# Local attention in groups of 32 queries: 64x32 and 128x32 TensorE tiles in place of 64x128 and 128x64

## The chip, the cores and the metric

One core of a Trainium2 chip runs the whole program. The metric is the device time of one execution in microseconds (us); the times shown are medians of several runs, and one further execution was profiled.

## What is computed

A block of attention feeds two feed-forward layers, all in fp32. Of 544 tokens in each of 4 batches, 32 are global and see every key, and 512 are local and see the 32 global keys and the local keys within 32 positions. There are 8 heads of 64.

```python
window, scale = 32, 1.0 / np.sqrt(D)                  # B, H, Sl, Sg, D = 4, 8, 512, 32, 64
sm = lambda s: e / (e.sum(-1) + 1e-9)                 # with e = exp(s - max(s))
out_g = sm(scale * q_g @ k_all.T) @ v_all             # k_all, v_all: global, then local
s_ll = where(abs(i - j) <= window, scale * q_l @ k_l.T, -1e9)
out_l = sm(concat(scale * q_l @ k_g.T, s_ll)) @ concat(v_g, v_l)
x = concat(out_g, out_l) as [2176 tokens, 512]
h = maximum(x @ w1_in, 0); x = (h * h) @ w1_out       # 512 -> 2048 -> 512
h = maximum(x @ w2_in, 0); out = (h * h) @ w2_out
```

## The kernel before

**Two stages.** First comes attention, with the first of the feed-forward work let in between; from about 168 us on there is feed-forward work alone. A feed-forward product is made of three fp32r matmuls, high by high, high by low and low by high parts (`three`, lines 580 to 583), of 384 or 512 moving columns each; the weights and activations are split into such parts by ScalarE (high) and VectorE (low).

**Local attention** is done by `pair(j)`, 32 times: two heads (e = 0, 1) of 256 queries, as two tiles (t = 0, 1) of 128 queries with 224 keys each (96 local ones, the 32 global ones, 96 local ones). For each pair the steps are these. (1) Three loads, issued by SyncE: keys `rk`, queries `rq` and values `vt` (two buffers). (2) `scores`: 4 matmuls of 64 rows by 128 columns with 224 moving keys, the two heads on the two halves of the rows, into banks S0 and S1. (3) On VectorE a custom operation adds the mask, scales, and takes the minimum (line 339), in 4 pieces; on ScalarE the exponential with the sum read out of the accumulator (line 344), in 4 pieces. (4) `tiny` turns the sums into reciprocals, and 4 passes over 224 columns multiply the weights by them (`copy("nm", ...)`, five of six on VectorE). (5) `trans`: 8 transposes on TensorE, of 128x128 and 96x96; ScalarE evicts them in 4 copies into `pt`. (6) `pv`: 8 matmuls of 64 columns with the weights moving (128 or 96 queries), the sum over keys in two parts (128 and 96 of them), into bank O0. It comes out transposed, as the feed-forward layer wants it. (7) `split_out` splits it into `xh` (ScalarE) and `xl` (VectorE).

An fp32 matmul of the code leaves two records in the trace, a transpose one.

**Global attention** is done by `glob(bb)`, four times: `scores` twice (line 425: 8 matmuls of 64x32, 272 moving keys), 11 transposes, and `pv` (line 475: 40 matmuls of 128x32 and 32x32, 64 values moving). Its keys and values are 2.5 MB of loads (`kg`, `y`).

**What sets the order.** All operations are first handed to `Plan`, which simulates them with booked costs and priorities (`add(engine, cost, priority, ...)`) and writes each engine's instructions in the order found. So costs, the `CFG` numbers and the buffer counts set the order, and each engine then runs its list strictly. SyncE issues the loads in list order too: one that waits for its buffer holds up those behind it.

**PSUM** has 8 banks: h0, h1, S0, S1, Y0, PT0, PT1 (transposes) and O0 (products with values).

**Weights** come as 8-byte numbers: `weight` loads 512 KB into one raw buffer and rebuilds fp32 on VectorE in 4 passes and one of AND (line 507) or, 5 times in 8, of Abs on ScalarE. **Activation** of hidden units (`activate`, line 590) of staged sums is relu, square and square again on ScalarE, or for one in six (`gs`) one VectorE pass and one ScalarE copy.

Of the kernel before, what the change touches and what calls it, by code (L numbers as in the profile page):

```python
# [17 lines left out]
S = SG + SL  # L18
# [6 lines left out]
NEAR = 96  # L25
# [10 lines left out]
CFG = {'warm': 27,  # L36
 'sg': 'A',
 'tl': 'DDDDD',
 'EARLY': 8,
 'nm': 'DDDADD',  # L40
 'ev': 'A',
 'yc': 'AAA',
 'wl': 'D',
 'gl': 'D',
 'xh': 'AA',
 'glob': [5.9, 15.73, 25.15, 42.23],
 'w0': 26.27364175797601,
 'w1': 9.640861192642154,
 'moe': [65.961, 79.468, 82.888, -1123.016, 96.609],
 'step': [0.0012, 0.0036, 0.0016, 0.0125, 0.102],  # L50
 'NK': 3,
 'NQ': 5,
 'wa': 'DAAAADDA',
 'lid': -5.887,
 'lmk': -15.028,
 'lead': 15.411,
 'NM': 1,
 'NS': 5,
 'NPT': 3,
 'NV': 2,  # L60
 'NR': 7,
 'NWR': 1,
 'NWT': 4,
# [3 lines left out]
 'PT': ['PT0', 'PT1'],  # L67
 'O': ['O0'],
 'tp': [215.87, 786.002, 884.208, 247.503],
 'order': ['A0B', 'BA0', 'AB0', 'A0B', 'AB0', '0BA', 'B0A', 'A0B', 'A0B', 'A0B', 'BA0', 'A0B', 'BA0', 'BA0'],  # L70
 'NSLOT': 9,
 'NGS': 2,
 'gf': 'A',
 'gs': 'AAAADA',
# [110 lines left out]

def switch(a, b):

    if a in "SVWX":
        return 0.0 if a == b else 0.095 if b in "SVWX" else 0.205 if b in "MG" else 0.145
    return 0.092 if b in "SVWX" else 0.012 if a != b else 0.0  # L190
# [10 lines left out]
def pe_r(n, m=128):  # L201
    return max(n + 32, 2 * m + 6) / 2400
# [3 lines left out]
def kernel(ctx: ExitStack, tc: tile.TileContext, kl, ql, vl, gk, gv, win, wout, msk, idn, out):  # L206
# [87 lines left out]
    cnt = {"S": 0, "PT": 0, "g": 0, "h": 0, "Y": 0, "r": 0, "x": 0}  # L294
# [10 lines left out]
    def pair(j, prio):  # L305
        u, h2 = divmod(j, H // 2)
        kb, qb, vb = j % NK, j % NQ, j % NV
# [7 lines left out]
        K, Q = ("rk", kb), ("rq", qb)  # L315
# [3 lines left out]
        load(prio - lead + 0.5, vt[vb], vl[j], 262144, A, (("v", vb),))  # L319
# [10 lines left out]
        add("PE", 0.77, P(), scores, A + (K, Q), tuple(sk), mode="S")  # L330
        pbs = []
        ok = CFG["O"][j % len(CFG["O"])]
        mb = j % NM
        for e in range(2):
            sb, s = (2 * j + e) % NS, sk[e]
            for t in range(2):
                qt = (u % 2) * 2 + t
                mi = 0 if qt == 0 else (2 if qt == 3 else 1)
                add("DVE", 0.32, P(), lambda t=t, mi=mi, sb=sb, s=s: nc.vector.tensor_tensor_reduce(  # L339
                    out=st[sb][:, t, :], in0=bank[s][:, t * WIN:(t + 1) * WIN], in1=masks[:, mi, :],  # L340
                    op0=ALU.add, op1=ALU.min, scale=-0.125, scalar=3.0e38, accum_out=mn[sb][:, t:t + 1]),
                    A + (s, "masks"), (("s", sb, t), ("mn", sb, t)))
            for t in range(2):
# [459 lines left out]
    for j in range(NI // 2):  # L803
        pair(j, 2 * j)
        for g, at in enumerate(GPOS):
            if at // 2 == j:
                glob(g, at + 0.5)
# [139 lines left out]
```

## Time and profile before

| | us |
|---|---|
| median of 3 runs (854.95 to 856.67) | 855.0 |
| the profiled execution | 854.51 |
| its span | 852.7 |
| TensorE busy | 842.1 (99%) |
| VectorE busy | 668.6 (78%) |
| ScalarE busy | 520.8 (61%) |
| load and store queues | 22.8% of 16 engines |

Busy time of TensorE is the union of records whose ends overlap the next one's start, so work is better read from start to start of neighbouring records. Rows of the timeline merge equal instructions that follow each other: "x16" is 16 records, and the second number is from the first start to the last end. The window view gives the busy time of each engine in a stretch, the granted TensorE clock (1.00 is 2.4 GHz), the mean busy share of the 16 DMA engines, and GB/s. The releaser named in brackets is what ended an idle time.

### The profile page before, as it was taken

What the parts mean: (1) busy time and instruction counts of PE and PEld (TensorE: products, weight loads), DVE (VectorE), ACT (ScalarE), POOL (GpSimd) and SP (SyncE); (2) the same over time, 40 slices, a digit from 0 to 9 for tenths busy, and PEclk for the clock granted to TensorE, in tenths of its full rate; (3) what the DMA queues carried; (4) which work ended last, traced back from release to release, by engine and by line L of the source; (5) the groups of instructions that cost most, each with busy time, mean ns of one, the idle gap of its engine ahead of it and who ended that gap; (6) DMA issues with size and microseconds to landing.
All of it is one profiled execution on the core that took longest, in us unless ns stands there. A gap on an engine that the chain in (4) does not pass through costs nothing.

```text
span 852.7 us, 14049 instructions
## 1 busy us (share of the span) xinstructions
PE 842.1 (99%) x5242; PEld 746.9 (88%) x5242; DVE 668.6 (78%) x1558; ACT 520.8 (61%) x1238; POOL 0.2 (0%) x4
## 2 busy tenths in 40 slices
PE   9899999999999999999999999999999999999998
PEld 7577777899989888989899898898989988998997
DVE  4889889616998888868887999779696987597554
ACT  6999999936765644454557777745364644465252
POOL 0000000000000000000000000000000000000000
PEclk9999999999999999999999999999999999999999
DMA  8776745200011111210211002112020112010023
GB/s 305 283 243 243 245 147 165 55 21 1 1 50 50 61 64 52 73 50 25 75 50 51 1 25 75 49 50 75 26 74 26 60 65 75 1 50 25 1 75 136
DMA packets 28580, 68.16 MB, mean 80 GB/s; under 512 B 3168, under 2 KB 13024, under 8 KB 28512
## 3 DMA queue, kind: packets, MB, share of 16 engines
q1 hardware_dynamic: 28512, 67.27, 22.8%
q8 instruction: 41, 0.67, 0.3%
q14 instruction: 27, 0.22, 0.1%
HBM read 62.80 MB, written 4.46 MB: 79 GB/s over the span
## 4 chain that ended last, share of the span: by engine, by line
PE 91%; DMA 3%; DVE 3%; ACT 2%; issue 1%; SPq 0%; ACTq 0%
PE h L581 8%; PE h L583 7%; PE h L582 7%; PE PT L583 6%; PE PT L582 6%; PE PT L581 6%; PE S L581 5%; PE S L583 5%; PE S L582 5%; PE Y L581 5%; PE Y L582 5%; PE Y L583 5%; PE O L583 3%; PE O L582 3%; PE O L581 3%; PE O L379 3%
## 5 line engine op out<-in xcount | busy, mean ns | idle before, releaser
L237 DVE TENSOR_TENSOR gl<-r,gh 128x384 fp32r<-128x384 f32 (+1 forms) x160 | 96.6, 609 | 78.7 <-ACT r L605 75.1
L581 PE MATMUL PT<-gh,whi 128*128 128x384 f32 (+1 forms) x288 | 102.5, 356 | 0.0
L582 PE MATMUL PT<-gl,whi 128*128 128x384 f32 (+1 forms) x288 | 102.4, 356 | 0.0
L583 PE MATMUL PT<-gh,wlo 128*128 128x384 f32 (+1 forms) x288 | 102.4, 356 | 0.0
L536 ACT ACTIVATE whi<-wt 128x512 fp32r<-128x512 f32 x92 | 57.3, 624 | 48.6 <-DVE wt L512 25.3
L602 ACT ACTIVATE gh<-r 128x384 fp32r<-128x384 f32 (+1 forms) x146 | 81.6, 562 | 8.6 <-PE O L583 5.0
L605 ACT ACTIVATE r<-r 128x384 f32<-128x384 f32 (+1 forms) x146 | 82.4, 567 | 4.0
L634 DVE TENSOR_TENSOR y<-y,PT 128x384 f32<-128x384 f32 (+1 forms) x130 | 75.7, 603 | 6.6 <-PE PT L583 6.5
L581 PE MATMUL h<-xh,whi 128*128 128x384 f32 (+1 forms) x216 | 79.6, 368 | 0.0
L583 PE MATMUL h<-xh,wlo 128*128 128x384 f32 (+1 forms) x216 | 77.9, 361 | 0.0
L237 DVE TENSOR_TENSOR wlo<-wt,whi 128x512 fp32r<-128x512 f32 x92 | 63.2, 687 | 18.6 <-ACT whi L536 18.4
L582 PE MATMUL h<-xl,whi 128*128 128x384 f32 (+1 forms) x216 | 77.6, 359 | 0.0
L581 PE MATMUL Y<-gh,whi 128*128 128x384 f32 (+1 forms) x208 | 76.4, 367 | 0.4 <-ACT y L222 0.2
L583 PE MATMUL Y<-gh,wlo 128*128 128x384 f32 (+1 forms) x208 | 74.9, 360 | 0.0
L582 PE MATMUL Y<-gl,whi 128*128 128x384 f32 (+1 forms) x208 | 74.8, 359 | 0.0
L601 ACT ACTIVATE r<-r 128x512 f32<-128x512 f32 (+1 forms) x70 | 40.2, 574 | 53.8 <-DVE r L711 53.7
L583 PE MATMUL S<-xh,wlo 128*128 128x384 f32 (+1 forms) x200 | 70.1, 350 | 0.0
L581 PE MATMUL S<-xh,whi 128*128 128x384 f32 (+1 forms) x200 | 70.0, 350 | 0.0
L582 PE MATMUL S<-xl,whi 128*128 128x384 f32 (+1 forms) x200 | 69.9, 350 | 0.0
L344 ACT ACTIVATE s<-s,mn 128x224 f32<-128x224 f32 x128 | 60.5, 475 | 8.0 <-DVE mn L339 5.0
L581 PEld LDWEIGHTS PT<-gh,whi 128*128 128x128 f32 x288 | 54.1, 188 | 4.5 <-ACT y L222 0.2
L583 PEld LDWEIGHTS PT<-gh,wlo 128*128 128x128 f32 x288 | 54.1, 188 | 4.5
(125 smaller groups left out, 1949.7 us busy)
## 6 DMA issues: line engine op xcount, KB each, us to landing
wraw<-win SPq DMA_DIRECT2D x32, 512.0 KB, 3.4
wraw<-wout SPq DMA_DIRECT2D x32, 512.0 KB, 3.4
v<-vl SPq DMA_DIRECT2D x32, 256.0 KB, 3.0
rk<-kl SPq DMA_DIRECT2D x32, 192.0 KB, 3.8
y<-gv SPq DMA_DIRECT2D x8, 640.0 KB, 7.2
kg<-gk SPq DMA_DIRECT2D x8, 576.0 KB, 5.9
rq<-ql SPq DMA_DIRECT2D x32, 128.0 KB, 3.8
out<-y SPq DMA_DIRECT2D x12, 192.0 KB, 1.9
```

The source lines that it names most:

```text
L237: add("DVE", dve(n), prio, lambda: nc.vector.tensor_tensor(out=get(out_), in0=get(a), in1=get(b), op=ALU.subtract), reads, writes, lock=True)
L344: add("Activation", 0.48, P(), lambda t=t, e=e, sb=sb: nc.scalar.activation(out=st[sb][:, t, :], in_=st[sb][:, t, :], func=AF.Exp, bias=mn ...
L379: nc.tensor.matmul(out=bank[ok][64 * e:64 * e + 64, 128 * t:128 * t + n], lhsT=vt[vb][0:n, 128 * k + 64 * e:128 * k + 64 * e + 64], rhs=pt ...
L536: nc.scalar.activation(out=whi[slot], in_=tf, func=AF.Copy)
L581: nc.tensor.matmul(out=out_, lhsT=hi, rhs=xhi, start=start, stop=False, skip_group_check=again)
L582: nc.tensor.matmul(out=out_, lhsT=hi, rhs=xlo, start=False, stop=False, skip_group_check=again)
L583: nc.tensor.matmul(out=out_, lhsT=lo, rhs=xhi, start=False, stop=stop, skip_group_check=again)
L601: add("Activation", act(nb), P(), lambda: nc.scalar.activation(out=r, in_=src, func=AF.Relu), (S,), (R,))
L602: add("Activation", act(nb) + 0.04, P(), lambda: nc.scalar.activation(out=a, in_=r, func=AF.Square), (R,), (("gh", f),))
L605: add("Activation", act(nb) + 0.04, P(), lambda: nc.scalar.activation(out=r, in_=r, func=AF.Square), (), (R,))
L634: add("DVE", dve(nb), P(), lambda: nc.vector.tensor_tensor(out=yd, in0=yd, in1=o, op=ALU.add), (yk[d],), (Y,))
```

## The change

Each tile of 128 queries is cut into 4 groups g of 32. A group sees only 128 of the 224 keys (from 32g on), so scores, mask, exponential and transposes are 128 wide in place of 224.

* `scores` becomes 16 matmuls of 64x32 with 128 moving keys; groups lie on the four column quarters, heads on the two row halves.
* The exponential no longer reads out a sum. The values get a column of ones (65 columns per head, 128 keys for each group), so the product yields the sum as well. The load of values grows from 256 KB to 520 KB a pair; the mask shrinks from 336 to 192 KB.
* `trans` is 4 transposes of 128x128 into one bank, evicted in 2 copies over the old scores; the 4 normalising passes are gone.
* `pv` is 16 matmuls of 128x32 in which the 65 values move, each complete in itself, with queries on the partitions.
* `tiny` and one multiplication of 256 columns (`og`) divide on VectorE, straight from PSUM; `back`, two transposes, turns the quotient round into the same bank O, from which `split_out` reads as before.
* PSUM: PT1 goes, a second O bank comes.
* `weight` clamps before it shifts (a max in place of a comparison and product at the end), and its first pass is on VectorE 5 times in 7.
* All staged activations go the VectorE way (`gs` is 'D'), and the other `CFG` numbers and booked costs differ, so that the order of all lists differs. Of first feed-forward matmuls the order now puts 132 ahead of the last product with values, where it put 186.

```diff
-WIN = 224
-NEAR = 96
+KEYS = 128
+VW = 2 * (D + 1)
...
- 'wa': 'DAAAADDA',
+ 'wa': 'DDDDADA',
...
- 'PT': ['PT0', 'PT1'],
- 'O': ['O0'],
+ 'PT': ['PT0'],
+ 'O': ['O0', 'O1'],
...
- 'gs': 'AAAADA',
+ 'gs': 'D',
...
         def scores():
             for t in range(2):
-                c, w = slice(128 * t, 128 * t + 128), slice(160 * t, 160 * t + WIN)
-                for e in range(2):
-                    r = slice(64 * e, 64 * e + 64)
-                    nc.tensor.matmul(out=bank[sk[e]][:, t * WIN:(t + 1) * WIN], lhsT=rq[qb][r, c], rhs=rk[kb][r, w],
-                                     start=True, stop=True)
+                for g in range(4):
+                    c, w = 128 * t + 32 * g, 160 * t + 32 * g
+                    for e in range(2):
+                        r = slice(64 * e, 64 * e + 64)
+                        nc.tensor.matmul(out=bank[sk[e]][32 * g:32 * g + 32, t * KEYS:(t + 1) * KEYS],
+                                         lhsT=rq[qb][r, c:c + 32], rhs=rk[kb][r, w:w + KEYS], start=True, stop=True)
...
-                copy("nm", P(), st[sb][:, t, :], st[sb][:, t, :], WIN, A + (("sm", mb, e, t),), (("s", sb, t),),
-                     scalar=sm[mb][:, e, t:t + 1])
...
+        def trans():
+            for k in range(4):
+                nc.tensor.transpose(bank[tk][:, 128 * k:128 * k + 128], st[sb][:, k, :], ident)
...
         def pv():
             for t in range(2):
-                for n, c in ((128, 1), (NEAR, 0)):
-                    k = 2 * t + c
-                    for e in range(2):
-                        nc.tensor.matmul(out=bank[ok][64 * e:64 * e + 64, 128 * t:128 * t + n],
-                                         lhsT=vt[vb][0:n, 128 * k + 64 * e:128 * k + 64 * e + 64],
-                                         rhs=pt[pbs[e]][0:n, t, 128 - 128 * c:128 - 128 * c + n], start=c == 1, stop=c == 0,
-                                         skip_group_check=True)
+                for e in range(2):
+                    for g in range(4):
+                        v = VW * (4 * t + g) + (D + 1) * e
+                        o = (D + 1) * (2 * t + e)
+                        nc.tensor.matmul(out=bank[ok][32 * g:32 * g + 32, o:o + D + 1],
+                                         lhsT=st[sb][:, 2 * e + t, 32 * g:32 * g + 32], rhs=vt[vb][:, v:v + D + 1],
+                                         start=True, stop=True)
...
+        def tiny():
+            nc.vector.tensor_scalar_add(out=sm[mb], in0=four[:, :, D:D + 1], scalar1=1e-9)
+            nc.vector.reciprocal(out=sm[mb], in_=sm[mb])
...
+        add("DVE", dve(256), P(), lambda: nc.vector.tensor_tensor(
+            out=og[ob].rearrange("p (k c) -> p k c", k=4), in0=four[:, :, 0:D], in1=sm[mb].to_broadcast([128, 4, D]), op=ALU.mult),
+            A + (ok, SM), (OG,))
...
+        def back():
+            for t in range(2):
+                nc.tensor.transpose(bank[ok][:, 128 * t:128 * t + 128], og[ob][:, 128 * t:128 * t + 128], ident)
...
-        add("DVE", dve(512), P(), lambda: nc.vector.scalar_tensor_tensor(
-            out=tf, in0=high.bitcast(F32), scalar=2.0 ** -15, in1=tf, op0=ALU.is_ge, op1=ALU.mult), (R,), (T,), lock=True)
...
+        add("DVE", dve(512, True), P(), lambda: nc.vector.tensor_scalar(
+            out=tf, in0=tf, scalar1=2.0 ** -15, scalar2=None, op0=ALU.max), (), (T,), lock=True)
```

**Order on TensorE, in attention.** Before, after the last transposes of the first global block (s are exponentials, pt evicted weights, v values):

```order
L363 MATMUL PT_152<-ident,s_126 128x128
L364 MATMUL PT_152<-ident,s_126 96x96
L363 MATMUL PT_152<-ident,s_126 128x128
L364 MATMUL PT_152<-ident,s_126 96x96
L379 MATMUL O_153<-pt_128,v_132 64x128
L379 MATMUL O_153<-pt_129,v_132 64x128
L379 MATMUL O_153<-pt_128,v_132 64x96
L379 MATMUL O_153<-pt_129,v_132 64x96
L379 MATMUL O_153<-pt_128,v_132 64x128
L379 MATMUL O_153<-pt_129,v_132 64x128
L379 MATMUL O_153<-pt_128,v_132 64x96
L379 MATMUL O_153<-pt_129,v_132 64x96
```

Now, somewhat past the first global block (L355 is `trans`, L369 `pv`, L387 `back`, L584 to L586 a feed-forward product):

```order
L369 MATMUL O_154<-v_130,s_122 32x65 x16
L355 MATMUL PT_152<-ident,s_124 128x128 x4
L584 MATMUL h_147<-xh_65,whi_99 128x512
L585 MATMUL h_147<-xl_70,whi_99 128x512
L586 MATMUL h_147<-xh_65,wlo_107 128x512
L369 MATMUL O_153<-v_131,s_123 32x65 x16
L387 MATMUL O_154<-ident,og_128 128x128 x2
L355 MATMUL PT_152<-ident,s_125 128x128 x4
```

One pair has 4 transposes where it had 8, 16 small products where it had 8, and two transposes more, which stand behind the next pair's product.

**Order on SyncE, at the loads of the second global block** (`kg`, `y`; wraw is a weight chunk). Before, they stand ahead of the values of the sixth pair:

```order
L302 DMA v_131<-vl 128x512
L302 DMA rk_116<-kl 128x384
L302 DMA rq_122<-ql 128x256
L302 DMA wraw_94<-win 128x1024
L302 DMA kg_139<-gk 128x1152
L302 DMA y_78<-gv 128x1280
L302 DMA rk_117<-kl 128x384
L302 DMA rq_118<-ql 128x256
L302 DMA kg_140<-gk 128x1152
L302 DMA y_74<-gv 128x1280
L302 DMA v_132<-vl 128x512
```

Now they stand ahead of the values of the ninth pair:

```order
L306 DMA rk_115<-kl 128x384
L306 DMA rq_119<-ql 128x256
L306 DMA v_131<-vl 128x1040
L306 DMA kg_140<-gk 128x1152
L306 DMA y_78<-gv 128x1280
L306 DMA y_74<-gv 128x1280
L306 DMA wraw_95<-win 128x1024
L306 DMA rk_116<-kl 128x384
L306 DMA rq_120<-ql 128x256
L306 DMA v_130<-vl 128x1040
L306 DMA kg_141<-gk 128x1152
```

The global loads moved three pairs back, and each load of values is twice as long.

**Order on VectorE, in the feed-forward stage** (L711 and L714 add into a staged sum r, L237 and L241 make low parts gl or wlo). Before:

```order
L237 TENSOR_TENSOR wlo_112<-wt_96,whi_104 128x512
L512 SCALAR_TENSOR_TENSOR wt_97<-wraw_94,wt_97 128x512
L711 TENSOR_TENSOR r_88<-r_88,S_149 128x512
L711 TENSOR_TENSOR r_87<-r_87,S_149 128x512
L237 TENSOR_TENSOR gl_84<-r_88,gh_80 128x512
```

Now:

```order
L714 TENSOR_TENSOR r_87<-r_87,S_150 128x512
L599 SCALAR_TENSOR_TENSOR r_87<-r_87 128x512
L510 TENSOR_SCALAR wt_97<-wt_97 128x512
L512 TENSOR_SCALAR wt_97<-wt_97 128x512
L241 TENSOR_TENSOR gl_84<-r_87,gh_80 128x512
```

A relu-and-square (L599) has come between the sum and the low part, 84 times in all where it was 14.

## Rows read from the trace of the kernel before

**Rows 1.** The page: TensorE busy, and DMA share in 40 slices.

```profile
PE 842.1 (99%) x5242; PEld 746.9 (88%) x5242; DVE 668.6 (78%) x1558; ACT 520.8 (61%) x1238; POOL 0.2 (0%) x4
DMA  8776745200011111210211002112020112010023
```

**Rows 2.** Timeline of TensorE, 60 to 70 us: start, length, then the instruction.

```profile
60.72 0.27 PE L363 MATMUL PT<-ident,s 128*128 128x128 f32 x1
60.83 0.25 PE L364 MATMUL PT<-ident,s 96*96 96x96 f32 x1
61.01 0.99 PE L379 MATMUL O<-pt,v 128*64 128x128 f32 x16
61.93 0.33 PE L363 MATMUL PT<-ident,s 128*128 128x128 f32 x1
62.10 0.25 PE L364 MATMUL PT<-ident,s 96*96 96x96 f32 x1
62.18 0.27 PE L363 MATMUL PT<-ident,s 128*128 128x128 f32 x1
...
62.47 1.03 PE L327 MATMUL S<-rk,rq 64*128 64x224 f32 x8
63.43 0.50 PE L581 MATMUL h<-xh,whi 128*128 128x512 f32 x1
63.77 0.39 PE L582 MATMUL h<-xl,whi 128*128 128x512 f32 x1
63.99 0.40 PE L583 MATMUL h<-xh,wlo 128*128 128x512 f32 x1
...
65.71 0.69 PE L425 MATMUL S<-kg 64*32 64x272 f32 x16
66.33 0.33 PE L363 MATMUL PT<-ident,s 128*128 128x128 f32 x1
```

**Rows 3.** Timeline of TensorE, 26 to 29 us: the global product.

```profile
27.05 1.46 PE L475 MATMUL O<-y,kg 128*32 128x64 f32 x80
28.43 0.84 PE L327 MATMUL S<-rk,rq 64*128 64x224 f32 x6
```

**Rows 4.** Timeline of TensorE: the first transposes and the last product with values.

```profile
10.48 0.27 PE L363 MATMUL PT<-ident,s 128*128 128x128 f32 x1
...
167.61 0.99 PE L379 MATMUL O<-pt,v 128*64 128x128 f32 x16
```

**Rows 5.** Windows: length, busy us of each engine, TensorE clock, DMA share, GB/s.

```profile
0.00:168.00 168.00, 162.22 (x1748) 123.67 (x1750) 135.79 (x582) 151.81 (x527) 0.20 (x4) 1.00 0.63 213
0.00:40.00 40.00, 35.22 (x389) 26.39 (x390) 27.42 (x130) 30.12 (x106) 0.20 (x4) 1.00 0.83 294
15.00:20.00 5.00, 4.15 (x59) 2.31 (x58) 3.35 (x14) 3.45 (x14) 0.00 (x0) 1.00 1.01 410
60.00:70.00 10.00, 10.00 (x105) 6.72 (x106) 9.39 (x43) 9.97 (x35) 0.00 (x0) 1.00 0.92 341
168.00:853.00 685.00, 679.88 (x3500) 623.22 (x3496) 532.85 (x976) 368.96 (x712) 0.00 (x0) 1.00 0.13 47
200.00:260.00 60.00, 59.48 (x310) 54.32 (x309) 59.12 (x111) 41.31 (x84) 0.00 (x0) 1.00 0.06 19
```

**Rows 6.** Groups by line and shape: busy us, mean ns, idle before.

```profile
L344 ACT ACTIVATION_READ_ACCUMULATOR s<-s,mn 128x1 f32 x128 | 24.6, 192 | 0.0
L227 DVE TENSOR_SCALAR s<-s,sm 128x224 f32<-128x224 f32 x107 | 29.2, 332 | 0.4
L394 DVE TENSOR_TENSOR xl<-O,xh 128x256 fp32r<-128x256 f32 x28 | 11.7, 418 | 3.6 <-ACT xh L222 3.4
L596 DVE SCALAR_TENSOR_TENSOR r<-r 128x384 f32<-128x384 f32 x8 | 4.4, 552 | 0.0
L596 DVE SCALAR_TENSOR_TENSOR r<-r 128x512 f32<-128x512 f32 x6 | 4.1, 688 | 0.1
```

**Rows 7.** Waits of TensorE from 168 us to the end, the longest.

```profile
PE h L581 <- ACT r L222: 0.4, 1, 0.4
```

More of the change, by code (lines that the diff above doesn't have):

```diff
@@ L35 @@
 STAGES = KF // 2
-CFG = {'warm': 27,
- 'sg': 'A',
- 'tl': 'DDDDD',
+CFG = {'warm': 17,
+ 'sg': 'AA',
+ 'tl': 'D',
  'EARLY': 8,
- 'nm': 'DDDADD',
- 'ev': 'A',
- 'yc': 'AAA',
+ 'ev': 'AAA',
+ 'yc': 'A',
  'wl': 'D',
  'gl': 'D',
[L45 to L50, printed above, removed]
- 'NK': 3,
- 'NQ': 5,
- 'wa': 'DAAAADDA',
[L54 to L59, printed above, removed]
+ 'xh': 'AAAAA',
+ 'glob': [11.02, 27.11, 43.12, 59.85],
+ 'w0': 1813.0042290862768,
+ 'w1': 707.3824610332841,
+ 'moe': [94.929, 87.982, 97.24, -1794.774, 111.976],
+ 'step': [0.005, 0.0157, 0.0024, 0.0026, 0.0014],
+ 'NK': 3,
+ 'NQ': 4,
+ 'wa': 'DDDDADA',
+ 'lid': -8.183,
+ 'lmk': -122.717,
+ 'lead': 63.237,
+ 'NM': 2,
+ 'NS': 6,
  'NV': 2,
- 'NR': 7,
+ 'NR': 8,
  'NWR': 1,
- 'NWT': 4,
+ 'NWT': 3,
  'Y': ['Y0'],
@@ L338, in pair @@
                 mi = 0 if qt == 0 else (2 if qt == 3 else 1)
[L339 to L343, printed above, removed]
-                add("Activation", 0.48, P(), lambda t=t, e=e, sb=sb: nc.scalar.activation(
-                    out=st[sb][:, t, :], in_=st[sb][:, t, :], func=AF.Exp, bias=mn[sb][:, t:t + 1], scale=-1.0,
-                    accum_out=sm[mb][:, e, t:t + 1]), A + (("mn", sb, t),), (("s", sb, t), ("sm", mb, e, t)))
@@ L348, in tiny @@
-        def tiny():
-            nc.vector.tensor_scalar_add(out=sm[mb], in0=sm[mb], scalar1=1e-9)
-            nc.vector.reciprocal(out=sm[mb], in_=sm[mb])
-        add("DVE", 0.3, P(), tiny, A, tuple(("sm", mb, e, t) for e in range(2) for t in range(2)), lock=True)
-        for e in range(2):
-            i = 2 * j + e
-            sb = i % NS
-            for t in range(2):
-                copy("nm", P(), st[sb][:, t, :], st[sb][:, t, :], WIN, A + (("sm", mb, e, t),), (("s", sb, t),),
-                     scalar=sm[mb][:, e, t:t + 1])
-            tk = take("PT", CFG["PT"])
-            def trans(sb=sb, tk=tk):
-                for t in range(2):
-                    nc.tensor.transpose(bank[tk][:, 256 * t:256 * t + 128], st[sb][:, t, NEAR:WIN], ident)
-                    nc.tensor.transpose(bank[tk][0:NEAR, 256 * t + 128:256 * t + 128 + NEAR],
-                                        st[sb][0:NEAR, t, 0:NEAR], ident[0:NEAR, 0:NEAR])
-            add("PE", 0.384, P(), trans, A + (("s", sb, 0), ("s", sb, 1), "ident"), (tk,), mode="T")
-            pb = i % NPT
-            two = bank[tk].rearrange("p (t c) -> p t c", t=2)
-            copy("ev", P(), pt[pb][:, :, 0:128], two[:, :, 0:128], 256, A + (tk,), (("pt", pb),), psum=True)
-            copy("ev", P(), pt[pb][0:NEAR, :, 128:128 + NEAR], two[0:NEAR, :, 128:128 + NEAR], 2 * NEAR, A + (tk,), (("pt", pb),), psum=True)
-            pbs.append(pb)
@@ new lines, in pair @@
+        tk = take("PT", CFG["PT"])
+        every = tuple(("s", sb, k) for k in range(4))
+        def trans():
+            for k in range(4):
+                nc.tensor.transpose(bank[tk][:, 128 * k:128 * k + 128], st[sb][:, k, :], ident)
+        add("PE", 0.45, P(), trans, A + every + ("ident",), (tk,), mode="T")
+        for e in range(2):
+            copy("ev", P(), st[sb][:, 2 * e:2 * e + 2, :], bank[tk][:, 256 * e:256 * e + 256].rearrange("p (k c) -> p k c", k=2),
+                 256, A + (tk,), every[2 * e:2 * e + 2], psum=True)
@@ L374, in pv @@
+        ok = take("O", CFG["O"])
         def pv():
             for t in range(2):
[L376 to L382 removed]
@@ L888, in _pack @@
             w = w.reshape(H // 2, 2, WIN, D).transpose(0, 2, 1, 3)
-            vl[u, :, 0:NEAR, t, 0] = w[:, 0:NEAR]
-            vl[u, :, :, t, 1] = w[:, NEAR:WIN]
+            for g in range(4):
+                vl[u, :, :, t, g, :, 0:D] = w[:, 32 * g:32 * g + KEYS]
     ka = np.concatenate([k_g, k_l], axis=2)
```

96 lines of the change are left out of this document (53 added, 43 removed).

## The prediction

> **What bounds the kernel now.** I read the page first: TensorE is busy 99% of the span, the loads 22.8%, and these are bunched in the first fifth of the slices [rows 1]. Then the windows: in the first 168 us, the attention stage, TensorE shares the load with ScalarE (151.8 us busy), VectorE (135.8) and the DMA engines (share 0.63); afterwards it is busy 680 of 685 us at clock 1.00 [rows 5]. The longest wait of TensorE after 168 us is 0.4 us [rows 7]. So the time is TensorE's own work, plus what it loses in attention. What a pair costs there is read from start to start, since records overlap [rows 2]: scores 62.47 to 63.43, 0.96 us; product with values 61.01 to 61.93, 0.92; a 128 transpose 60.72 to 60.83, 0.11; a 96 one 0.09, so 0.78 for eight. Sum 2.66, and 85.1 for 32 pairs. Entering tiles of less than the full array costs 0.09 more (60.83 to 61.01, against 0.09 within transposes); leaving them costs 0.05 to a transpose (61.93 to 62.10 against 0.11) and 0.11 to a feed-forward product (63.43 to 63.77 against 0.22) [rows 2]. The order has 53 entries, 33 leaves to transposes and 17 to products: 8.3. A global block is two scores of 0.62 (65.71 to 66.33) [rows 2], a product of 1.38 (27.05 to 28.43) [rows 3] and 11 transposes of 0.11: 15.3 for four. The 186 feed-forward matmuls ahead of the last product with values, most at 0.23 (63.77 to 63.99, the thinner fewer), are some 41. Together 149.7. The last product with values starts at 167.6 [rows 4], so the stage loses 18: the first transposes come only at 10.5 [rows 4], and of the first 40 us TensorE is busy 35, with the DMA engines at 0.83 [rows 5].
>
> **Scores, products, transposes.** These are the terms that lie on the path. A round is what runs abreast. Two clocks a column at 2.4 GHz are 0.83 ns. The old scores are 8 records two abreast, 4 rounds of 224 columns, 0.75 us, and 0.21 remain. The global scores have the very tile of the new ones, 64x32: 16 records eight abreast, 2 rounds of 272, 0.45; 0.17 remain [rows 2]. The global product has the tile of the new one, 128x32: 80 records four abreast, 20 rounds of 64, 1.07; 0.31 remain for two drains, as it changes its tile once [rows 3]. So a drain costs 0.16, whatever the tile. New scores: 32 records, 4 rounds of 128, 0.43 + 0.17 = 0.60. New product: 32 records, 8 rounds of 65, 0.43 + 0.16 = 0.59. Transposes: 4 of 0.11, and 2 of 0.11 for `back`, 0.67. A pair is 1.86 in place of 2.66, and 32 of them 59.5 in place of 85.1: **25.6 us less**. Entries are 53 again, leaves 37 and 15: nothing. For the product the other end is the old one's round, 0.11 for 128 columns: 8 rounds are 0.88 + 0.17, 0.46 more a pair, 14.7 in all. I take the low end, since the tile and nearly the width are those of L475; 65 is odd, which no row shows.
>
> The Trainium skill, "TensorE: Matmul & The Clock Gate", section "Wait — 56ns, not 53.3ns?", speaks against this: start to start of matmuls never falls below about 25 ns, however few the columns. L475 shows 80 in 1.38 us, 17 ns each, drains included [rows 3], so the trace doesn't agree for tiles abreast. By that floor of the Trainium skill the new scores and the new product would be 0.80 + 0.16 each, an estimate, and the 25.6 would shrink to 2 us.
>
> **Transfers.** Each load of values grows by 270 KB, 8.65 MB in all; ten weight chunks of 512 KB stand ahead of the last load of values in the new order, where the old had twelve, and the mask is 0.15 MB less. The DMA engines worked 0.63 x 168 = 106 us in the stage, at 213 / 0.63 = 338 GB/s of busy time; with long rows they reached 410 / 1.01 = 406 [rows 5]. The growth is thus 21.3 to 25.6 us, I take 23.5 (rows of 4 KB lie between); 1.2 MB less are 3.5 off. Need: 126 us by the last load of values. TensorE's own work to there is 59.5 + 8.3 + 15.3 + 30 (132 feed-forward matmuls) = 113. So **the transfers become the longer of the two**, and with two value buffers a load waits for a product and the product for a load. At share 1.0 the last product could start at 126, at the 0.92 of a good stretch at 137, at the 0.83 of the first 40 us at 152 [rows 5]. I take 137, since the global blocks now come later and the opening is less crowded, though SyncE's list still waits in order. TensorE then loses 24 where it lost 18: **6 us back**. The ends are -3 (work and loads nearly hidden, 128) and +21 (152). The 11 us of feed-forward work that the stage gives away only move behind it.
>
> **VectorE and ScalarE in attention.** Off the path. VectorE loses 29.2 us of normalising [rows 6] and a part of its mask passes, and gains 32 divisions of 256 columns from PSUM at the 0.42 of L394, 13.4 [rows 6]: 135.8 [rows 5] falls to some 120 or less in a stage of 137. ScalarE loses at least the 24.6 of readouts [rows 6], of 151.8: its hold on the stage goes, and that leaves the loads next.
>
> **The way back.** New waits: `back` waits for sum, reciprocal and division, and the bank O is held through them, some 1 us; TensorE is strictly in order, so all that stands behind `back` would wait. The order puts the next pair's product or transposes between them, 0.45 us and more, and there are two O banks. I take 0; without the cover it is up to 0.5 a pair, 16 us, of which the wait for loads would hide the most. One PT bank in place of two: four transposes, two evictions, about 1 us of a 4 us pair, 0.
>
> **Feed-forward stage.** The matmuls are the same 3672. The staged activations move 70 more passes to VectorE, 34 of 0.55 and 36 of 0.69 [rows 6], 43.5 us, on 532.9 of 685 [rows 5]: 78% to 84%. ScalarE loses more than that. The last product's place to a waiting TensorE has been nil [rows 7], so I take 0, up to the rival below. Fewer dummy matmuls at the start fill idle time: 0.
>
> **Sum.** 854.5 (profiled) - 25.6 + 6 = 834.9; the median of the runs shown lies 0.5 above the profiled one: **835 us**.
>
> **Rivals.** *Transfers hide* (0.20): the early crowding of the old order was what cost the 18, and it eases as much as the loads grow; 854.5 - 25.6 = 829. For it: the global loads stand behind the eighth pair now. Against it: 126 of need over 113 of work. *Transfers bind as in the first 40 us* (0.15): share 0.83 throughout, 854.5 - 25.6 + 21 = 850. For it: two value buffers and one list. Against it: that stretch held two global blocks. *Issue binds* (0.04), the slower end: the small matmuls go out one by one at the pace of the global scores, (0.62 - 0.17) / 16 = 0.028 each [rows 2], whatever their width. Scores and product then cost 32 x 0.028 + 0.17 = 1.07 each, a pair 2.81, 4.8 more in all than before, and the loads are hidden: 859. It turns slower from 0.026 on; against it speak the 17 ns of L475 [rows 3]. The floor of 25 ns in the Trainium skill's page "TensorE: Matmul & The Clock Gate" would be this mechanism just short of that point, some 853 as an estimate. *VectorE binds the feed-forward stage* (0.03): between 200 and 260 us it is busy 59.1 of 60 [rows 5]. If all 43.5 landed on TensorE, 878; slower from 20 on, nearly half of it. Against: each new pass takes the place of two of ScalarE's in the same chain. *It doesn't run abreast in the new order*, eight score tiles as two: 12 more rounds of 0.11, above 870; in the 0.04 too. No net change for other reasons: 0.02.
>
> **How the numbers follow.** Forecast 835 with 0.56, its own range 829 to 844 (share 0.87 to 1.0, part of the product's upper end). The range, 826 to 848, adds the hidden case and half of the bound one. Measurements of this kernel tell 0.2% (1.7 us) from no change: faster 0.90, same 0.03, slower 0.07.
>
> **What would show it.** The scores 0.60 and products 0.59 from start to start; the last product with values near 137 us, the DMA share of the stage above 0.88, and waits of TensorE and of SyncE's list that name the loads of values. After it, the feed-forward stage should last 696 us, no wait above 1 us. Wrong it would be if a round took over 0.06 us in the product, if TensorE waited for `og`, or if the stage after attention grew.

## The result and the profile after

The changed kernel takes 841.7 us (median of 4 runs, 840.24 to 842.66), the kernel before, run beside it, 855.4 (4 runs, 854.95 to 856.67): a ratio of 0.984, 95% interval 0.982 to 0.986. The forecast was 835, range 826 to 848. The sign and the range held; of the 20 us forecast, 14 came. The profiled execution took 842.18, its span 840.4.

The page of the changed kernel, section by section: busy time of each engine, then two lines of the 40 slices (granted clock of TensorE, share of the DMA engines), then the DMA queues with packets, MB and share. It answers [rows 1].

```profile
PE 816.3 (97%) x6438; PEld 725.9 (86%) x6438; DVE 669.2 (80%) x1575; ACT 397.8 (47%) x863; POOL 0.2 (0%) x4
...
PEclk8999999999999999999999999999999999999999
DMA  9889896100012112111120011211111102110023
...
q1 hardware_dynamic: 28512, 75.77, 26.1%
q8 instruction: 50, 0.82, 0.4%
```

TensorE is busy 25.8 us less, yet the span is 12.3 shorter: it stands still for more of it, 24 us against 10.6. Where, the windows tell (columns as in [rows 5]; 146.6 is the start of the last product with values):

```profile
0.00:146.60 146.60, 126.72 (x2864) 92.19 (x2864) 99.03 (x496) 99.06 (x295) 0.20 (x4) 0.97 0.85 296
...
0.00:40.00 40.00, 31.84 (x727) 22.96 (x728) 22.53 (x128) 24.24 (x73) 0.20 (x4) 0.91 0.89 312
40.00:100.00 60.00, 54.86 (x1207) 39.03 (x1206) 45.00 (x221) 45.36 (x132) 0.00 (x0) 1.00 0.90 319
100.00:140.00 40.00, 33.63 (x793) 25.02 (x793) 26.95 (x134) 25.99 (x81) 0.00 (x0) 0.96 0.80 273
...
168.00:841.00 673.00, 668.37 (x3441) 614.96 (x3440) 562.47 (x1063) 288.27 (x548) 0.00 (x0) 1.00 0.14 48
```

In the first 140 us TensorE idles 19.7 us while the DMA engines are at 0.80 to 0.90; afterwards it is busy 668 of 673. Before, it was busy 59.0 of 60 us between 40 and 100 and 60.0 of 60 between 100 and 160:

```profile
40.00:100.00 60.00, 59.01 (x685) 44.48 (x685) 52.99 (x221) 57.94 (x198) 0.00 (x0) 1.00 0.72 248
100.00:160.00 60.00, 59.99 (x614) 45.85 (x612) 51.21 (x224) 55.78 (x202) 0.00 (x0) 1.00 0.48 149
```

So before, with a share of 0.72 and then 0.48, the transfers had room. The waits of TensorE in the changed kernel, over the whole span (sum, count, longest), say what it waits for:

```profile
PE O L369 <- DMA v<-vl: 7.2, 5, 2.4
PE S L332 <- issue: 3.2, 2, 1.6
PE h L584 <- issue: 2.4, 1, 2.4
PE S L332 <- DMA rq<-ql: 2.0, 3, 1.6
...
PE O L387 <- DVE og L381: 0.6, 2, 0.4
```

Two kinds lead: values that have not landed, and "issue", where nothing that the profile shows was waited for. A stop of the second kind, and what came before and after it, in the timeline of TensorE (start, length, instruction, idle before it):

```profile
12.13 0.77 PE L355 MATMUL PT<-ident,s 128*128 128x128 f32 x4 [0.69 <-DMA ident<-idn]
12.82 1.10 PE L332 MATMUL S<-rk,rq 64*32 64x128 f32 x32
13.86 1.09 PE L369 MATMUL O<-v,s 128*32 128x65 f32 x32
14.88 1.12 PE L355 MATMUL PT<-ident,s 128*128 128x128 f32 x4
15.93 0.62 PE L332 MATMUL S<-rk,rq 64*32 64x128 f32 x18
18.10 0.45 PE L332 MATMUL S<-rk,rq 64*32 64x128 f32 x14 [1.55 <-issue]
```

The scores at 15.93 stop after 18 of their 32 records, in the middle of one operation whose data are there. The scores at 12.82 take 1.04 us to the next start, the product 1.02; the granted clock there is at its lower level, as shown in the last section. Undisturbed, both cost what the prediction gave them. The same view at 64 us, which answers [rows 2]:

```profile
63.72 0.66 PE L458 MATMUL PT<-ident,kg 128*128 128x128 f32 x4
64.30 0.66 PE L369 MATMUL O<-v,s 128*32 128x65 f32 x32
64.90 0.67 PE L332 MATMUL S<-rk,rq 64*32 64x128 f32 x32
65.50 0.44 PE L387 MATMUL O<-ident,og 128*128 128x128 f32 x2
```

Four transposes 63.72 to 64.30, 0.58 with the entry into tiles (0.53 by the forecast); product 64.30 to 64.90, 0.60; scores 64.90 to 65.50, 0.60. The last product with values, which answers [rows 4]:

```profile
146.63 0.67 PE L369 MATMUL O<-v,s 128*32 128x65 f32 x32
```

From this the time divides in two, in spans: the stage to the last product 167.6 to 146.6, minus 21.0; the rest 685.1 to 693.8, plus 8.7, as 132 feed-forward matmuls are done ahead where 186 were; sum 12.3. With TensorE's own work of 113 to that place, the forecast's sum, it loses 33.6 us there (an estimate, as all losses below). The forecast had 24, before it was 18.

### The profile page after: what moved, and what is told of

Read it like the earlier page. It is cut to its first block, busy times and chain, and to the rows that moved or that the text cites. A ratio compares the mean times of both kernels' runs of the same rounds, so it can differ in the third digit from the quotient of the medians.

```text
span 840.4 us, 15941 instructions
## 1 busy us (share of the span) xinstructions
PE 816.3 (97%) x6438; PEld 725.9 (86%) x6438; DVE 669.2 (80%) x1575; ACT 397.8 (47%) x863; POOL 0.2 (0%) x4
## 2 busy tenths in 40 slices
DMA packets 28585, 76.78 MB, mean 91 GB/s; under 512 B 3168, under 2 KB 13152, under 8 KB 28512
## 3 DMA queue, kind: packets, MB, share of 16 engines
q1 hardware_dynamic: 28512, 75.77, 26.1%
## 4 chain that ended last, share of the span: by engine, by line
PE 90%; DMA 5%; DVE 2%; issue 1%; ACT 1%; SPq 1%
PE h L584 8%; PE h L586 8%; PE h L585 8%; PE O L584 7%; PE O L586 7%; PE O L585 7%; PE S L586 5%; PE S L585 5%; PE S L584 5%; PE Y L584 5%; PE Y L585 5%; PE Y L586 5%; DMA v<-vl 4%; PE PT L586 3%; PE PT L584 3%; PE PT L585 3%
## 5 line engine op out<-in xcount | busy, mean ns | idle before, releaser
L241 DVE TENSOR_TENSOR gl<-r,gh 128x384 fp32r<-128x384 f32 (+1 forms) x160 | 96.9, 608 | 46.4 <-PE Y L585 16.5
L585 PE MATMUL O<-gl,whi 128*128 128x384 f32 (+1 forms) x288 | 102.5, 356 | 0.0
L586 PE MATMUL O<-gh,wlo 128*128 128x384 f32 (+1 forms) x288 | 102.5, 356 | 0.0
L584 PE MATMUL O<-gh,whi 128*128 128x384 f32 (+1 forms) x288 | 102.5, 356 | 0.0
L584 PE MATMUL h<-xh,whi 128*128 128x384 f32 (+1 forms) x232 | 85.0, 366 | 2.4 <-issue 2.4
L637 DVE TENSOR_TENSOR y<-y,O 128x384 f32<-128x384 f32 (+1 forms) x130 | 76.2, 603 | 10.0 <-PE O L586 9.9
L601 ACT ACTIVATE gh<-r 128x512 fp32r<-128x512 f32 (+1 forms) x84 | 48.5, 577 | 72.8 <-DVE r L599 68.8
L586 PE MATMUL h<-xh,wlo 128*128 128x384 f32 (+1 forms) x232 | 82.7, 356 | 0.0
L241 DVE TENSOR_TENSOR wlo<-wt,whi 128x512 fp32r<-128x512 f32 x92 | 62.6, 686 | 23.6 <-ACT whi L539 23.3
L584 PE MATMUL Y<-gh,whi 128*128 128x384 f32 (+1 forms) x208 | 75.5, 363 | 0.2 <-ACT y L226 0.2
L586 PE MATMUL Y<-gh,wlo 128*128 128x384 f32 (+1 forms) x208 | 74.8, 360 | 0.0
L226 ACT ACTIVATE r<-h 128x512 f32<-128x512 f32 (+1 forms) x57 | 31.7, 555 | 89.5 <-PE h L586 87.7
L586 PE MATMUL S<-xh,wlo 128*128 128x384 f32 (+1 forms) x184 | 65.4, 356 | 0.0
L584 PE MATMUL S<-xh,whi 128*128 128x384 f32 (+1 forms) x184 | 65.3, 355 | 0.0
L585 PEld LDWEIGHTS O<-gl,whi 128*128 128x128 f32 x288 | 54.1, 188 | 4.6
L584 PEld LDWEIGHTS O<-gh,whi 128*128 128x128 f32 x288 | 54.1, 188 | 4.5
L586 PEld LDWEIGHTS O<-gh,wlo 128*128 128x128 f32 x288 | 54.1, 188 | 4.4
L599 DVE SCALAR_TENSOR_TENSOR r<-r 128x512 f32<-128x512 f32 (+1 forms) x84 | 52.0, 619 | 0.7
```

The costliest lines, as they stand in the source:

```text
L226: add("Activation", act(n) + (0.0 if psum else 0.13 if key == "nm" else 0.04), prio, lambda: nc.scalar.activation(out=out_, in_=in_, func= ...
L241: add("DVE", dve(n), prio, lambda: nc.vector.tensor_tensor(out=get(out_), in0=get(a), in1=get(b), op=ALU.subtract), reads, writes, lock=True)
L584: nc.tensor.matmul(out=out_, lhsT=hi, rhs=xhi, start=start, stop=False, skip_group_check=again)
L585: nc.tensor.matmul(out=out_, lhsT=hi, rhs=xlo, start=False, stop=False, skip_group_check=again)
L586: nc.tensor.matmul(out=out_, lhsT=lo, rhs=xhi, start=False, stop=stop, skip_group_check=again)
L599: add("DVE", dve(nb), P(), lambda: nc.vector.scalar_tensor_tensor(out=r, in0=r, scalar=0.0, in1=r, op0=ALU.max, op1=ALU.mult), (), (R,), l ...
```

## The experiments

The question is what makes the 33.6. **Theory A**: the transfers fill the DMA engines, and TensorE waits for them. **Theory B**: the chain through VectorE and ScalarE, the order, or two buffers for values. Below, "after" is the changed kernel, 841.7 us with its last product at 146.6; times of runs are medians, ratios are to the kernel before on the same chip.

**A quarter of the bytes, on both kernels** (`few_bytes` from after, `before_few` from before):

```diff
-load(prio - lead, rk[kb], kl[j], 196608, A, (K,))
+load(prio - lead, rk[kb][:, 0:96], kl[j][:, 0:96], 196608, A, (K,))
 (rq, vt, kg and the values of glob alike; the rest of each tile is zeroed once at the start)
```

> Every attention load (queries, keys, values, both global blocks) brings only the first quarter of its columns; the rest of each tile holds zeros, so scores and products are computed from the wrong numbers. The order of all instructions and the number of transfers are those of the changed kernel; some 28 MB less are moved in the first 145 us. Theory A, full DMA engines: what TensorE loses ahead of the last product with the values (about 33 us, its own work there being 113) comes from transfers, whether as a wait for a tile, as a stop in the middle of an operation while an instruction packet lands late, or as a halved clock after such a stop. Then the last product starts at 120 to 127 instead of 146.6, there are hardly any stops of more than 0.8 us, the granted clock stays at 1.00 after the opening, and the time is 816 to 823. Theory B, the chain through VectorE and ScalarE (mask, exponential, exits) or the order: the last product stays at 137 or later and the time at 832 or more.

> The kernel before, with the first quarter of the columns of every attention load (queries, keys, values, both of a global block), the rest of the tiles being zeros, so that the attention is computed from the wrong numbers; order unchanged. Theory A, full DMA engines are what the change met and the kernel before hardly did: before lost 18 us to its last product with the values, the changed kernel with a quarter of the bytes still 14, so before loses 2 to 5 us less and takes 850 to 853. Rival B, transfers cost before as much as they cost the changed kernel (19 us), so that they explain nothing of the difference: 835 to 840.

From after: 823.07 us (822.87 to 823.20), ratio 0.961 (0.959 to 0.963). From before: 852.53 (851.86 to 854.82), ratio 0.996 (0.994 to 0.997). The windows of the first and its last product, then its longest waits of TensorE:

```profile
0.00:40.00 40.00, 35.70 (x869) 25.50 (x871) 26.65 (x153) 28.86 (x88) 6.43 (x17) 1.00 0.51 145
40.00:100.00 60.00, 59.21 (x1440) 42.66 (x1440) 50.34 (x245) 50.34 (x152) 0.00 (x0) 1.00 0.41 115
...
127.41 0.67 PE L369 MATMUL O<-v,s 128*32 128x65 f32 x32
...
PE O L799 <- DVE warm L797: 1.0, 1, 1.0
PE O L387 <- DVE og L381: 0.7, 2, 0.4
...
PE S L332 <- issue: 0.4, 1, 0.4
```

The last product of the second:

```profile
164.94 0.99 PE L379 MATMUL O<-pt,v 128*64 128x128 f32 x16
```

Theory A, a hair past the upper edge of what was expected of the first (823.07 for 816 to 823, 127.4 for 120 to 127) and inside what was expected of the second. With the same order, the same instructions and the same number of packets (28512), the last product comes at 127.4: 14.4 us lost instead of 33.6, so **19 us hung on transfers**. Neither a stop for "issue" above 0.4 us nor, to the last product, a granted clock below 1.00 is left. The kernel before gains 2.7 us to its last product (167.6 to 164.9): with a quarter of the bytes both kernels lose 14 to 15 us, and the opening before the first transposes, 10.5 us in [rows 4], is the largest part of that. Theory B would have left the last product late; no wait for VectorE or ScalarE sums to more than 1.0.

**Half of the values** (`half_v`): 8.5 MB less, so that values move the bytes of the kernel before.

```diff
-load(prio - lead + 0.5, vt[vb], vl[j], 128 * 32 * VW, A, (V,))
+load(prio - lead + 0.5, vt[vb][:, 0:4 * VW], vl[j][:, 0:4 * VW], 128 * 32 * VW, A, (V,))
```

> The changed kernel with the second half of each value tile not loaded (two buffers are zeroed once instead), every list in the same order; half of the local outputs are wrong for it. It moves 8.5 MB less. Theory A (the transfers pace attention): the last product with values starts at 126 to 131 us instead of 146.6, the time falls by 14 to 20 us to 822 to 828. Theory B (TensorE loses its time to its own order, to code that comes late and to the halved clock, whatever the loads do): last product at 143 or later, time 838 or more.

833.95 us (830.34 to 835.92), ratio 0.973 (0.970 to 0.976). The window to its last product and its longest waits:

```profile
0.00:138.80 138.80, 125.52 (x2864) 91.00 (x2864) 98.73 (x496) 98.30 (x295) 1.20 (x6) 0.98 0.75 252
...
PE S L332 <- DMA rk<-kl: 2.9, 1, 2.9
PE h L584 <- issue: 1.9, 1, 1.9
```

The last product moves 7.8 us, between the two theories. The grown values are thus 8 of the 19 us. The other 11 are there with the old bytes, which cost the kernel before only 2.7: nearly the same transfers (35.0 MB and 35.8 by rate and length of the windows), in 139 us instead of 168, at a share of 0.75 instead of 0.63. That the shorter time is what makes them dear is argued; the order differs as well. A wait for values no longer leads, waits for keys and for "issue" do (a second stop for "issue", at L332, is 1.7).

**The opening** (`small_glob`): the first global block's 2.4 MB cut to an eighth.

```diff
+n = 144 if bb == 0 else 1152
-load(prio - 3 + 0.05 * g, K[g][:, 0:1152], gk[2 * bb + g], 589824, A, (GK[g], GP[g]))
+load(prio - 3 + 0.05 * g, K[g][:, 0:n], gk[2 * bb + g, :, 0:n], 589824, A, (GK[g], GP[g]))
 (the values of the block alike)
```

> The first global block's four loads (2.4 MB, issued among the first pairs' loads) bring an eighth of their columns; the rest of the tiles holds zeros, so that block's result is wrong. Order unchanged, 2.1 MB less in the first 25 us. Theory A, the opening is crowded by the first global block: the product of the third pair starts near 19 to 20 instead of 25.9, the last one near 140 instead of 146.6, and the time is 834 to 836. Rival B, transfers set the pace all the way, so that time gained early is only waited for later: the third pair's product is early, but the last one starts only 0 to 2 us earlier, 840 to 842. Rival C, the instruction packets and the halved clock make the opening: the third pair's product stays at 24 or later, and so does everything else.

839.33 us (837.08 to 842.06), ratio 0.979 (0.976 to 0.982), which overlaps that of after. The third pair's product comes at 25.4 instead of 25.9, the last at 146.4. Rival C: the global loads do not make the opening late. Its stop and the wait list:

```profile
14.78 0.62 PE L332 MATMUL S<-rk,rq 64*32 64x128 f32 x18
17.40 0.56 PE L332 MATMUL S<-rk,rq 64*32 64x128 f32 x14 [2.00 <-issue]
...
PE S L332 <- issue: 5.7, 5, 2.0
```

The scores stop after the same 18 records as in after. A stop that keeps its place in the program while data come earlier points to the instructions themselves; the last section follows this up. The DMA queues of the first 15 us agree (share of 16 engines last), first after, then with a quarter of the bytes:

```profile
q1 hardware_dynamic: 2485, 4.48, 85.6%
```

```profile
q1 hardware_dynamic: 3244, 2.22, 53.0%
q8 instruction: 1, 0.02, 0.4%
```

With free engines a packet of the instruction queue has come by 15 us; with engines at 0.86 none has.

**Buffers for values** (`three_v`): a third one for the first 18 pairs, in room that is unused until then.

```diff
+vtj = [vt[0], vt[1], yflat[3][:, 0:8 * VW]][j % 3] if j < 18 else vt[j % 2]
-load(prio - lead + 0.5, vt[vb], vl[j], 128 * 32 * VW, A, (V,))
+load(prio - lead + 0.5, vtj, vl[j], 128 * 32 * VW, A, (V,))
```

> The changed kernel, same order and same bytes, but for the first 18 pairs the values rotate through three buffers in place of two (the third lies in a feed-forward tile not yet in use). Theory A1 (what paces is the bytes): the 18th product with values, at 90.6 us, comes at most 2 us earlier, time within 2 us of 841.7. Theory A2 (what paces is the two buffers, each load waiting for a product): the 18th product is 6 us or more earlier, time 836 or less.

839.35 us (834.46 to 841.40), ratio 0.979 (0.975 to 0.982); the 18th product at 91.1 (after 90.6), the last at 146.4. The time is 0.4 us further from 841.7 than theory A1 allowed, and the products come no earlier: the buffers do not set the pace.

**Loads booked slower** (`plan330`), so that the planner lays the order for 330 GB/s:

```diff
-reads, writes, tail=nbytes / 360e3)
+reads, writes, tail=nbytes / 330e3)
```

> The changed kernel with one number of the planner: loads are booked at 330 GB/s in place of 360, so that all lists are ordered for slower transfers. If the stage is long because the order was made for transfers faster than they are: more feed-forward work stands in the stage, the last product with values stays at 145 to 150, and the time falls by 3 to 6 us to 836 to 839. If the order is not what costs: 840 to 844.

842.87 us (841.26 to 846.24), ratio 0.984 (0.982 to 0.987): the time of after. In its trace 150 feed-forward matmuls instead of 132 stand ahead of the last product, which comes at 150.4. What moves ahead is given back behind; the loss stays.

**More work for TensorE** (`pe_plus`): two matmuls of 128 columns ahead of each product, on data that nobody reads.

```diff
 def pv():
+    for _ in range(2):
+        nc.tensor.matmul(out=bank[ok][:, 0:128], lhsT=warm, rhs=warm, start=True, stop=True)
```

> The changed kernel with two idle matmuls of 128 columns more on TensorE ahead of each product with values, same order: 32 x 2 x 0.21 = 14 us of work, and with the changes of tile some 17. If TensorE's own work is what the attention stage lasts: 855 to 859. If the transfers are: the work falls into TensorE's idle time, 842 to 849, and the last product with values at 147 to 154.

847.99 us (847.20 to 849.64), ratio 0.990 (0.988 to 0.992). Its window to the last product:

```profile
0.00:152.60 152.60, 141.33 (x2993) 108.45 (x2993) 101.09 (x496) 99.93 (x296) 0.20 (x4) 0.97 0.82 288
```

TensorE is busy 14.6 us longer than in the same window of after, and its last product comes 6.0 later. The rest went into time in which it had waited, as was expected if transfers set the pace (842 to 849). In this stage a microsecond of TensorE is worth less than half.

**Fewer bytes, everything computed** (`shift3`, `shift7`, `shift312`). The four windows of 128 keys of a half overlap by 96. `shift7` loads windows 0 and 3 and makes 1 and 2 from them, `shift3` loads three and makes window 2; both with the third buffer. GpSimd copies between partitions (destination window and partition, source, first partition, count):

```diff
-load(prio - lead + 0.5, vt[vb], vl[j], 128 * 32 * VW, A, (V,))
+load(prio - lead + 0.5, vtj[:, 0:6 * VW], vl[j], 128 * 24 * VW, A, (V,))
+for n, (d, s0, r, m) in enumerate(SHIFT):          # shift3: ((3, 0), 0, 64, 64), ((3, 64), 1, 32, 32), ((3, 96), 1, 64, 32)
+    add("Pool", 0.3, prio - lead + 0.6 + 0.01 * n, lambda d=d, s0=s0, r=r, m=m: nc.gpsimd.tensor_copy(
+        out=vtj[d[1]:d[1] + m, 2 * VW * d[0]:2 * VW * d[0] + 2 * VW],
+        in_=vtj[r:r + m, 2 * VW * s0:2 * VW * s0 + 2 * VW]), A + (V,), (("vc", vb, n),))
```

> Computes everything. Of the four overlapping windows of values of a half, three are loaded (390 KB a pair instead of 520) and GpSimd, idle until now, makes the fourth from two of them in three copies a pair; a third buffer for values for the first 18 pairs; the planner orders it with these copies in it. Theory A, bytes of values pace the attention: 4.3 MB less at the 312 GB/s that the engines moved is some 13 us of transfers, and by the run with half of the values (8.5 MB, 8 us) that is worth 4 us: 836 to 838. Rival B: the copies lengthen the way from the load to the product, or take VectorE's time, and it comes out at 841 or later.

> Computes everything. Two of the four windows of values are loaded (260 KB a pair, as in the kernel before) and GpSimd makes the other two in seven copies a pair; a third buffer for values for the first 18 pairs. Theory A, bytes of values pace the attention: as with half of the values left out, 832 to 835, and the last product before 141. Rival B: seven copies a pair, if each takes 0.4 us, are 2.8 us of the 4.4 us that a pair takes, and with their starts they become what the product waits for: last product at 147 or later, 842 or more.

`shift3`: 840.23 us (839.27 to 840.84), ratio 0.981 (0.979 to 0.983). `shift7`: 855.55 (854.25 to 858.06), ratio 0.999 (0.997 to 1.000), the gain all gone. GpSimd's copies in `shift7`, by shape (busy us, mean ns of one):

```profile
L329 POOL COPY v<-v 32x260 f32<-32x260 f32 x156 | 71.3, 457 | 7.4
...
L329 POOL COPY v<-v 64x260 f32<-64x260 f32 x26 | 11.1, 425 | 42.2 <-DMA v<-vl 38.5 <-PE S L437 1.9 <-PE O L377 0.8
```

Seven at 0.46 and 0.42 are 3.2 us a pair, behind each load and ahead of each product, and the longest wait of TensorE names them:

```profile
PE O L377 <- POOL v L329: 12.6, 11, 2.4
```

Its last product comes at 160.3. Rival B, for `shift7`. `shift3`, with three copies, lies between its theories; 2 us under after, not clearly.

> Computes everything. The changed kernel with a third buffer for values for the first 18 pairs (known to the planner), loads booked at 312 GB/s, as the trace of the changed kernel shows, instead of 360, and the planner's numbers for places (global blocks, early weights, feed-forward work, engines of small steps) set anew under that rate. Theory A: the transfers' 137 us ahead of the last product stay, but more feed-forward work stands in the places where TensorE waited, so that it loses 24 to 28 us to the last product instead of 33.6: 832 to 836. Rival B: as with loads booked at 330, an order written for slower loads changes nothing, 839 to 843.

> Computes everything. As the kernel with three loaded windows and one that GpSimd makes, with loads booked at 312 GB/s and the planner's numbers set anew under that rate. Theory A, both gains add up (4.3 MB less to move, and an order that fits the transfers): 830 to 834. Rival B: the copies' way from load to product costs what the bytes save, 838 to 842.

`new312` (after with the third buffer, loads booked at 312 GB/s, and the planner's numbers for global blocks, early weights and feed-forward work set anew for it): 840.02 us (838.36 to 843.03), ratio 0.982 (0.979 to 0.985): by time rival B. By its trace theory A has half a point: with 192 feed-forward matmuls ahead, 60 more than after (some 14 us at 0.23), the last product comes at 154.5, so that execution loses some 28 us, not 33.6; but its time, 838.36, is the lowest of four, and the median is not clearly below after. An order made for these transfers may be worth a few us; no run shows more. `shift312` (`shift3` treated so): 837.26 us (834.94 to 840.45), ratio 0.978 (0.974 to 0.981), the best of those that compute everything, and below after by an interval that barely clears it; it lies between its two theories; its last product comes at 149.1, with more feed-forward work ahead of it.

## Why the prediction came out as it did

**TensorE's own work: right.** Scores 0.60 as forecast, product 0.60 against 0.59, so 25.6 us less; 65 odd columns cost what the rate of 64 gave. The upper end of the product (1.05) is out. Between `few_bytes` and `before_few`, where transfers are out of the way, the profiled spans differ by 28.7 us (850.1 to 821.4): the 25.6, 0.8 that the stage loses less, and 2.2 that the feed-forward stage is shorter than the 696 forecast.

**No floor at issue: right.** 32 records in 0.60 us are 19 ns each, at four or eight abreast. The floor of about 25 ns in the Trainium skill, "TensorE: Matmul & The Clock Gate", section "Wait — 56ns, not 53.3ns?", does not hold here, for tiles abreast; by it scores and product would have cost 0.96 each, an estimate.

**The bytes: right.** 126 us of DMA time were forecast by the last load of values; 0.85 of the 146.6 us to the last product are 125. That transfers become the longer of the two was right too.

**What they cost TensorE: the step that failed.** "TensorE then loses 24 where it lost 18: 6 us back." It lost 33.6: 15.6 back. The term took a share of 0.92 for the whole stage from ten good microseconds of [rows 5], and got 0.85, 0.80 in the windows from 100 to 140. It took the loss as the excess of transfer time over work, as if what remained overlapped wholly. It did not here, with both nearly full: a late tile stops TensorE, which keeps strict order, and the DMA engines are not full throughout either, as SyncE's list waits for buffers that TensorE still reads. Of SyncE's waits in the first 146 us, the largest in sum is for the scores that read keys and queries:

```profile
SPq L306 <- PE S L332: 15.3, 15, 3.1
```

That such waits are what leaves the DMA engines idle is argued, not isolated. Between the two traces, stops of TensorE above 0.8 us ahead of the last product, not counting its first start, went from none to eight of 14.1 us in all. Five of them, 8.5 us, wait for data. Three, 5.6 us, wait for instructions, and the lower clock takes some 4 more (both in the last section): two terms that the sum did not have. The three together make 18 of the 19 us that hung on transfers. That the two new ones come to what the forecast missed, 9.6, is one trace's arithmetic, since a stop also lets the transfers catch up. The forecast's reason for the good value, that the opening is less crowded because the global blocks come later, failed as well. Only the later blocks moved: the first one's loads were issued at 8.1 to 11.2 us before and at 8.4 to 13.1 after. The first 40 us have a share of 0.89 where they had 0.83, the third pair's product comes at 25.9 where it came at 22.9, and taking those global loads away changes that by half a microsecond. With all attention loads cut to a quarter it comes at 20.3, with half of the values alone at 26.1: loads do make the opening late, but neither the first global block nor half of the values does it alone, and which loads do was not told apart.

**The loads' growth is half of it.** I charged the change for 8.65 MB. `half_v` shows that as 8 us; some 11 more are there with the old bytes, as the pairs come faster (argued above, not isolated).

**The rest of the stage: right.** VectorE is 99 us busy to the last product, under the 120 forecast, and ScalarE 99; `back` waits for `og` 0.6 us in all; the single PT bank shows in no wait above 0.5.

**The feed-forward stage: right.** It takes 693.8 us where 696 was forecast, and why it is 2.2 shorter was not looked into: that part of the result is luck. TensorE has no wait of 0.2 us or more after 168, with VectorE at 562 of 673 us, 84% as forecast. So neither that rival nor issue binds. Of the rivals, "transfers bind as in the first 40 us" names the mechanism; its 850 took the share lower than it came. So the mechanism was right, and the term for the stage's loss was sized 9.6 us too low; the 2.2 above and the width of the range kept 841.7 inside it.

## To carry to other kernels

When a change makes one engine's work shorter in a stage, compare what the DMA engines must move with the new length of the stage before counting the gain: here a share of 0.63 that hid nearly everything became 0.85, at which nearly 16 of 26 us went. A share taken from a good stretch is no price for a stage: here 126 us of transfers beside 113 us of work, in strict order on both sides, took 146.6. Where they are nearly full, look at the instructions too, which here came through the same engines. To test whether transfers are the cause, cut the columns of the loads and keep all instructions in order, on both kernels.

## What the hardware showed beyond this

**The clock fell in the middle of a busy stage.** In the kernel before, the granted clock is 1.00 in every window of [rows 5]; after, it is at the lower of its two levels in stretches, in windows (the last three numbers are clock, DMA share and GB/s):

```profile
12.00:16.00 4.00, 3.87 (x80) 2.71 (x87) 2.14 (x17) 2.93 (x10) 0.00 (x0) 0.57 1.02 383
16.00:20.00 4.00, 2.45 (x69) 1.66 (x70) 1.35 (x11) 1.71 (x6) 0.00 (x0) 0.91 1.01 398
20.00:24.00 4.00, 3.81 (x59) 2.39 (x58) 2.25 (x12) 2.74 (x10) 0.00 (x0) 0.66 1.04 397
...
115.00:120.00 5.00, 2.63 (x69) 2.03 (x68) 1.62 (x12) 3.04 (x12) 0.00 (x0) 0.83 1.01 389
120.00:125.00 5.00, 5.00 (x53) 3.89 (x53) 3.10 (x10) 2.09 (x6) 0.00 (x0) 0.83 1.03 395
```

Each follows a stop of TensorE: 1.55 us up to 10.76 and 0.69 up to 12.13, then 1.55 up to 18.10, and 2.37 up to 118.51, where the timeline reads

```profile
118.51 1.09 PE L369 MATMUL O<-v,s 128*32 128x65 f32 x32 [2.37 <-DMA v<-vl]
119.53 0.80 PE L584 MATMUL h<-xh,whi 128*128 128x512 f32 x1
```

A product that takes 0.60 takes 1.02 there. Scores, product and transposes from 12.82 to 15.93 took 3.1 us where they take 1.8 (0.60, 0.60, 0.58): 1.3 us lost in a stretch, some 4 in the three, an estimate from these rows. So a stop can be paid twice. Not every stop has it: those up to 40.6 and 47.6 left the clock at 1.00 in the window from 40 to 100. Nor is every slow operation the clock: in `few_bytes` the scores at 9.05 take 1.02 us to the next start, at 10.07, in the window from 0 to 40 whose granted clock is 1.00; why is open.

```profile
9.05 1.09 PE L332 MATMUL S<-rk,rq 64*32 64x128 f32 x32 [0.66 <-DVE mn L342]
```

The Trainium skill, "TensorE: Matmul & The Clock Gate", section "HAM oscillation — how this bites in real kernels", tells of the same, waits for DMA that let the clock fall so that the next group starts slow; the trace agrees for the stops up to 12.13 and 118.51, and after the one up to 18.10 the same follows a wait for instructions.

**Instructions come through the DMA engines too.** The changed kernel runs 6438 records on TensorE where 5242 ran, each with a weight load of its own, and 50 packets of its instruction queue arrive (16 KB each, from the page above) where 41 did:

```profile
q8 instruction: 41, 0.67, 0.3%
```

That is 258 weight loads and matmuls to a packet now (12876 in 50) and 256 before (10484 in 41). The stops for "issue" keep to this count. Number TensorE's instructions through the trace, weight loads, matmuls and semaphore instructions alike: in the changed kernel the stops for "issue" of 0.25 us or more in the attention stage stand at 448, 1471, 1728, 3007 and 4287. There are 42 such stops in the traces of the changed kernel and its ten variants, and every one stands 191 or 192 past a multiple of 256; the waits that name a tile are spread over all remainders. `pe_plus`, which puts more instructions ahead, moves the place in the program and keeps the number: 1471 falls among a pair's scores in after, in a global product in `pe_plus`.

```profile
40.61 0.49 PE L332 MATMUL S<-rk,rq 64*32 64x128 f32 x17 [1.64 <-issue]
```

```profile
39.70 0.27 PE L481 MATMUL O<-y,kg 32*32 32x64 f32 x2 [0.80 <-issue]
```

In after TensorE goes on 1.2 to 1.5 us behind the landing of a packet, at all five stops. So these are late instructions, not data: with the engines full they stop TensorE for up to 2.4 us, in the middle of an operation (18.10, 40.61) or ahead of one (47.60), and with a quarter of the bytes the only one left of that size, 0.4 us, stands at 1727. Three of the eight long stops of after are of this kind. What more or fewer instructions at the same bytes would cost, no run shows.
